# Four Fourier/GEGLU layers: transposed rows through a wide tile and memory, statistics by ScalarE, GELU as one ScalarE function

## The chip, the cores and the metric

The kernel runs on one core of one Trainium2 chip. Such a core has a matmul engine (TensorE, PE in the profile, with its weight load as PEld), VectorE (DVE), ScalarE (ACT), GpSimd (POOL) and SyncE (SP), which here only issues transfers. They work from one on-chip memory of 128 partitions; matmuls write to eight banks of an accumulator (PSUM), and transfers to and from the large memory run on 16 DMA engines. Each engine takes its own instructions in order, and waits on semaphores for the others. The metric is device time in microseconds (us) for one execution; lower is better.

## The reference

A row tensor x of 2048 x 512 passes through four layers. Each normalises its rows (mean and variance over 512, no learned factors) and adds its result to x.

```python
def _A_ref(x, dft_seq_re, dft_seq_im, dft_hid_re, dft_hid_im):      # layers 0 and 2
    a = einsum("bsd,ed->bse", x, dft_hid_re)
    b = einsum("bsd,ed->bse", x, dft_hid_im)
    return einsum("ts,bse->bte", dft_seq_re, a) - einsum("ts,bse->bte", dft_seq_im, b)
def _B_ref(x, w_gate, w_up, w_down):                                # layers 1 and 3
    return (_gelu(x @ w_gate) * (x @ w_up)) @ w_down
x = x + _A_ref(_layernorm(x), ...)
x = x + _B_ref(_layernorm(x), ...)
x = x + _A_ref(_layernorm(x), ...)
x = x + _B_ref(_layernorm(x), ...)
```

The sequence matrices are 2048 x 2048, the hidden ones 512 x 512, the gate and up weights 512 x 1792, the down weights 1792 x 512, all float32. GELU is the tanh form.

## The kernel before, in words

**Precision.** A float32 product is made of three matmuls on a faster type. Each operand is split into a high part (ScalarE copies it to that type, line 110) and a low part (VectorE takes the difference, line 111); `mm3` (lines 144 to 146) multiplies high by high, high by low and low by high into one bank. So nearly every tile that TensorE uses has first passed ScalarE and VectorE, or was stored split.

**Fewer products.** The sequence matrices and the gate/up weights are cut into 2 x 2 blocks and multiplied by Winograd's scheme of seven products in place of eight. The sums and differences of blocks this needs are VectorE's (lines 132 and 135): S1 to S4 on one side, T1 to T4 on the other.

**Layers 0 and 2** (`mix`) work on four blocks `b` of 512 output rows. Stages A11, A12, S2, S3 and A22 multiply sequence tiles by normalised rows; hidden stages then multiply by the hidden matrix, and `x_add` adds x and stores the rows. `plan` gives the order. In each stage of `six`, one step is six matmuls.

**Layers 1 and 3** (`geglu`) work on two halves `w` of 1024 rows, each as two parts of 512. For every `n` of 14 column groups, `up` makes seven products; `finished` applies GELU to the gate (`activated`, lines 719 to 726: square and tanh on ScalarE, two combined operations on VectorE) and multiplies by up. `down_steps` multiplies by the down weights: twelve matmuls each, six of them behind for part 0, and all 14 of part 1 after the ups.

These products need the normalised rows with the 512 features on the partitions, that is, transposed. `block_steps` makes them: `normed` normalises a row tile of 128 x 512 (VectorE statistics, POOL's power -0.5, VectorE's shift, ScalarE's scaling); `turned` (line 450) has TensorE transpose four 128 x 128 pieces into one bank; `first` and `second` copy and split from there, `fourth` and `divide` make and split the T sums.

**Order.** Two mechanisms set it, and a planner that knows assumed durations orders each engine's instructions by them. `items` lists every tile that a product will take, in order; `take` keeps up to five items split (`AHEAD`) and four more loaded (`RAW`) ahead of the product in hand, on SP's queue. `queue` is a list of side work: `step` runs its next entry after each step of the mix or each down step. Into it go the normalisations for the next layer, the transposes, the splitting of down weights (`down_weight_steps`, during layer 0) and of the gate/up weights (`weight_steps`, in layers 0 and 1; six entries a group, of which the first loads and the second sums). Split weights are stored by POOL's queue and read back by SP's.

**Buffers.** All 128 x 512 tiles come from 102 numbered slots (`NSLOT`), given out in the order in which they came free. A load into a slot waits for the slot's last reader. PSUM banks are given out likewise.

## Time and profile before

| | us |
|---|---|
| median of 3 runs | 1665.11 |
| lowest, highest | 1663.8, 1665.39 |
| profiled execution, its own time | 1666.76 |
| span of the profiled execution (first to last instruction) | 1664.9 |

| engine | busy us | share of the span |
|---|---|---|
| TensorE matmul | 1650.4 | 99% |
| TensorE weight load | 1359.2 | 82% |
| VectorE | 1190.7 | 72% |
| ScalarE | 776.2 | 47% |
| GpSimd | 169.3 | 10% |

The mean granted clock of TensorE is 0.998 of full speed. The transfers move 388.46 MB, on average 233 GB/s. How to read it: a busy matmul engine is not one at its best pace, as matmuls are pipelined and their ends are modelled, so a count of matmuls per stretch of time says more than a busy share. In a row of a group, the numbers after the bar are the summed busy time in us, the mean of one in ns, and the idle time of the engine before them with what ended it. In the windows view each row is a stretch of the span. In the view of waits each row is an engine's line, what it waited for, the sum in us, how often, and the longest.

The layers can be placed by the transfers: layer 0 lasts to about 390 us, layer 1 to about 840, layer 2 to about 1240, layer 3 to the end.

### The profile page before, as it was taken

What the parts mean: (1) busy time and instruction counts of PE and PEld (TensorE: products, weight loads), DVE (VectorE), ACT (ScalarE), POOL (GpSimd) and SP (SyncE); (2) the same over time, 40 slices, a digit from 0 to 9 for tenths busy, and PEclk for the clock granted to TensorE, in tenths of its full rate; (3) what the DMA queues carried; (4) which work ended last, traced back from release to release, by engine and by line L of the source; (5) the groups of instructions that cost most, each with busy time, mean ns of one, the idle gap of its engine ahead of it and who ended that gap; (6) DMA issues with size and microseconds to landing.
All of it is one profiled execution on the core that took longest, in us unless ns stands there. A gap on an engine that the chain in (4) does not pass through costs nothing.

```text
span 1664.9 us, 22527 instructions
## 1 busy us (share of the span) xinstructions
PE 1650.4 (99%) x7296; PEld 1359.2 (82%) x7296; DVE 1190.7 (72%) x2132; ACT 776.2 (47%) x1352; POOL 169.3 (10%) x288
## 2 busy tenths in 40 slices
PE   9999999999999999999999999999999999999999
PEld 6877788888788888888888888888888888888887
DVE  8997978687887765655898785857946556656561
ACT  7744434255565543534663333444635443444440
POOL 3212100021422110000210000000100000100000
PEclk9999999999999999999999999999999999999999
DMA  9788886778766876555665766565695559755551
GB/s 361 247 279 329 306 317 227 253 252 291 273 229 215 292 269 233 172 189 198 216 227 182 240 228 228 168 227 188 225 386 184 171 177 321 259 178 175 186 183 51
DMA packets 200726, 388.46 MB, mean 233 GB/s; under 512 B 23840, under 2 KB 27424, under 8 KB 200608
## 3 DMA queue, kind: packets, MB, share of 16 engines
q1 hardware_dynamic: 183168, 329.86, 59.1%
q0 software_dynamic: 17440, 57.16, 9.1%
q8 instruction: 58, 0.95, 0.2%
q14 instruction: 60, 0.49, 0.1%
HBM read 328.73 MB, written 58.20 MB: 232 GB/s over the span
## 4 chain that ended last, share of the span: by engine, by line
PE 93%; DVE 3%; DMA 2%; issue 1%; ACT 1%; SPq 0%; DVEq 0%; ACTq 0%
PE p L144 31%; PE p L145 30%; PE p L146 30%; DMA s<-wgu 2%; DVE s L111 1%; PE p L551 1%; PE p L454 1%; DVE s L135 1%; DMA s<-ws 1%; DVE s L132 1%; DMA s<-x 0%; DVE s L725 0%; DVE s L739 0%; DVE s L723 0%; ACT s L110 0%
## 5 line engine op out<-in xcount | busy, mean ns | idle before, releaser
L145 PE MATMUL p<-s,s 128*128 128x512 f32 x2368 | 921.7, 390 | 1.9 <-DVE s L111 1.9
L146 PE MATMUL p<-s,s 128*128 128x512 f32 x2368 | 908.6, 390 | 0.0
L144 PE MATMUL p<-s,s 128*128 128x512 f32 x2368 | 901.2, 391 | 7.0 <-DVE s L135 3.9
L110 ACT ACTIVATE s<-s 128x512 fp32r<-128x512 f32 (+1 forms) x758 | 438.0, 617 | 467.6 <-DVE s L132 98.6
L111 DVE TENSOR_TENSOR s<-s,s 128x512 fp32r<-128x512 f32 (+1 forms) x758 | 490.2, 679 | 87.1 <-ACT s L110 64.3
L144 PEld LDWEIGHTS p<-s,s 128*128 128x128 f32 x2368 | 445.0, 188 | 102.9 <-DVE s L135 5.0
L145 PEld LDWEIGHTS p<-s,s 128*128 128x128 f32 x2368 | 445.4, 188 | 95.0 <-DVE s L111 3.1
L146 PEld LDWEIGHTS p<-s,s 128*128 128x128 f32 x2368 | 445.2, 188 | 93.7 <-DVE s L111 0.7
L135 DVE TENSOR_TENSOR s<-s,p 128x512 f32<-128x512 f32 x316 | 213.0, 685 | 188.9 <-PE p L146 140.6
L139 ACT ACTIVATE s<-p 128x512 f32<-128x512 f32 x248 | 145.2, 593 | 187.4 <-PE p L146 171.4
L132 DVE TENSOR_TENSOR s<-s,s 128x512 f32<-128x512 f32 (+1 forms) x290 | 172.4, 608 | 23.4 <-DMA s<-ws 15.4
L722 ACT ACTIVATE s<-s 128x512 f32<-128x512 f32 x112 | 70.4, 630 | 91.7 <-DVE s L135 90.9
L725 DVE SCALAR_TENSOR_TENSOR s<-s,s 128x512 f32<-128x512 f32 x112 | 76.8, 690 | 38.2 <-ACT s L724 37.6
L378 POOL TENSOR_TENSOR rstd<-rstd,power 128x1 f32<-128x1 f32 x64 | 50.8, 803 | 506.7 <-DVE rstd L377 500.8
L723 DVE SCALAR_TENSOR_TENSOR s<-s,s 128x512 f32<-128x512 f32 x112 | 77.0, 690 | 33.5 <-ACT s L722 31.3
L724 ACT ACTIVATE s<-s 128x512 f32<-128x512 f32 x112 | 69.5, 627 | 25.0 <-DVE s L723 24.4
L135 DVE TENSOR_TENSOR s<-s,s 128x512 f32<-128x512 f32 (+1 forms) x78 | 50.1, 645 | 38.5 <-DMA s<-ws 22.1
L169 POOL DMA_DIRECT2D x<-s x48 | 26.1, 543 | 443.8 <-DVE s L135 440.8
L382 ACT ACTIVATE s<-s,shift,rstd 128x512 f32<-128x512 f32 x64 | 50.4, 811 | 36.5 <-DVE shift L380 32.1
L739 DVE SCALAR_TENSOR_TENSOR s<-s,s 128x512 f32<-128x512 f32 x84 | 58.0, 690 | 1.6
L197 POOL DMA_DIRECT2D wb<-s x84 | 45.2, 540 | 121.6 <-ACT s L110 85.1
L373 DVE BATCH_NORM_STATS2 st<-s 128x6 f32<-128x512 f32 x64 | 42.7, 689 | 19.8 <-DMA s<-x 19.8
(32 smaller groups left out, 254.6 us busy)
## 6 DMA issues: line engine op xcount, KB each, us to landing
s<-ws SPq DMA_DIRECT2D x432, 256.0 KB, 4.0
s<-wb SPq DMA_DIRECT2D x294, 256.0 KB, 4.1
s<-wd SPq DMA_DIRECT2D x224, 256.0 KB, 4.3
s<-x SPq DMA_DIRECT2D x126, 256.0 KB, 4.1
s<-wh SPq DMA_DIRECT2D x120, 256.0 KB, 4.8
wb<-s POOLq DMA_DIRECT2D x98, 256.0 KB, 3.5
x<-s POOLq DMA_DIRECT2D x48, 256.0 KB, 4.1
wd<-s POOLq DMA_DIRECT2D x28, 256.0 KB, 4.9
```

Source lines behind the costliest of these rows:

```text
L110: nc.scalar.activation(hi, src, AF.Copy)
L111: nc.vector.tensor_tensor(lo, src, f32(hi), op=ALU.subtract)
L132: nc.vector.tensor_tensor(out, a, b, op=ALU.subtract)
L135: nc.vector.tensor_tensor(out, a, b, op=ALU.add)
L139: nc.scalar.activation(v, src, AF.Copy)
L144: nc.tensor.matmul(ps, ah, bh, start=start, stop=False, skip_group_check=True)
L145: nc.tensor.matmul(ps, ah, bl, start=False, stop=False, skip_group_check=True)
L146: nc.tensor.matmul(ps, al, bh, start=False, stop=stop, skip_group_check=True)
L722: nc.scalar.activation(t, g, AF.Square)
L723: nc.vector.scalar_tensor_tensor(t, t, 1.0 / GELU_C, g, op0=ALU.add, op1=ALU.mult)
L724: nc.scalar.activation(t, t, AF.Tanh, scale=GELU_A * GELU_C)
L725: nc.vector.scalar_tensor_tensor(t, t, 1.0, g, op0=ALU.add, op1=ALU.mult)
```

## The change

Six things change together.

1. **Transposes.** TensorE's transposes go. VectorE transposes each normalised row tile in blocks of 32 x 32 into a quarter of a `wide` tile of 128 x 2048 (a pool of one buffer). When four rows are in, POOL's queue stores it to memory (1 MB). Later `fetch` reads it back with SP's queue, so that the features come to stand on the partitions: 32 transfers of 64 KB a block of rows. `first` and `second` split from those tiles; the copies from PSUM go.
2. **Order of rows.** This gives the 512 rows of a part an order of their own: tile n of a part holds four runs of 32 rows, one from each of the part's row tiles. The feed-forward layers load and store x so (`load_rows`, `add_rows` and `last_downs` pass `True` for `mixed`), and x is held in memory as four tensors of 512 rows a layer rather than sixteen of 128. The last four row tiles before layer 2 stay on the chip in that order, so layer 2 reads its last four sequence tiles of each half in it (`seq_tile`).
3. **Statistics.** From layer 1 on, ScalarE makes the sum and the sum of squares about the mean in the passes of a copy and a square, POOL two small operations, ScalarE the shift; layer 0 keeps VectorE's. Eight rows for layer 2 get theirs ahead (`terms_ahead`), during the second half of layer 1.
4. **GELU.** One ScalarE function in place of four operations; the factor 0.5 falls away.
5. **Weights.** Down weights are split at their first use in layer 1 rather than from the queue in layer 0. The loads of gate/up weights are issued a group ahead of the entries that sum and split them. Stored down weights are taken at most two items ahead (`NEAR`), loaded four.
6. **Places in the queue.** In the mix, the norms for the next layer enter in block 2, four in S2 and four in S3, with an empty step between; fetches, splits and T sums stay in the last block. In the feed-forward layers, a step of the queue also runs after every product, and the next half's rows enter before the last six downs of part 0. Slots: 98, so that the wide tile finds room.

```diff
-NSLOT = 102
+NSLOT = 98
...
-    nc.scalar.activation(warm, warm, AF.Tanh)
+    nc.scalar.activation(warm, warm, AF.Gelu_apprx_tanh)
...
+    def rows(layer, i, mixed=False):
+        g, n = divmod(i, NT)
+        if mixed:
+            return xs[layer, g].rearrange("(n j t) d -> j n t d", n=NT, t=32)[n]
+        return xs[layer, g][n * P:(n + 1) * P]
+
+    def x_load(layer, i, mixed=False):
         t = sb.get()
-        nc.sync.dma_start(t, xs[layer, i])
+        nc.sync.dma_start(t, rows(layer, i, mixed))
...
-        engine.dma_start(xs[layer + 1, i], t)
+        engine.dma_start(rows(layer + 1, i, mixed), t)
...
+            if stream["loaded"] > n + NEAR and items[stream["loaded"]][2] is whole:
+                break
...
+            if items[stream["split"]][2] is whole and stream["split"] > n + NEAR:
+                break
...
+    def make_down_first(f):
+        def run(v):
+            p = plain(v)
+            kept(wds[f], p)
+            return p
+        return run
...
+    def seq_tile(layer, n, k):
+
+        if layer and k >= NS - NT:
+            return ws[(n + 1) * NS - NT:(n + 1) * NS, (k % NT) * 32:(k % NT + 1) * 32]
+        return ws[n * NS + k]
...
+    def norm_terms(layer, i, x, junk):
+
+        pool = spool if layer == 0 else kpool
+        rstd = pool.tile([P, 1], F32, name="rstd")
+        shift = pool.tile([P, 1], F32, name="shift")
+        if layer == 0:
+            st = spool.tile([P, 6], F32, name="st")
+            nc.vector.bn_stats(st, x)
+            mv = spool.tile([P, 2], F32, name="mv")
+            nc.vector.bn_aggr(mv, st)
+            nc.vector.tensor_scalar_add(rstd, mv[:, 1:2], EPS)
+            nc.gpsimd.tensor_tensor(rstd, rstd, power, op=ALU.pow)
+            nc.vector.scalar_tensor_tensor(shift, mv[:, 0:1], -1.0, rstd, op0=ALU.mult, op1=ALU.mult)
+        else:
+
+            total = spool.tile([P, 1], F32, name="total")
+            mean = spool.tile([P, 1], F32, name="mean")
+            nc.scalar.activation(junk, x, AF.Copy, accum_out=total)
+            nc.scalar.activation(mean, total, AF.Copy, scale=-1.0 / D)
+            nc.scalar.activation(junk, x, AF.Square, bias=mean, accum_out=rstd)
+            nc.gpsimd.tensor_scalar(rstd, rstd, 1.0 / D, EPS, op0=ALU.mult, op1=ALU.add)
+            nc.gpsimd.tensor_tensor(rstd, rstd, power, op=ALU.pow)
+            nc.scalar.activation(shift, mean, AF.Copy, scale=rstd)
+        return rstd, shift
+
+    def terms_ahead(layer, i):
+        x, junk = x_load(layer, i), sb.get()
+        known[layer, i] = norm_terms(layer, i, x, junk)
+        sb.put(x, junk)
...
+                z = normed(layer, w * 2 * NT + i)
+                part, n = divmod(i, NT)
+                if n == 0:
+                    wide[part] = tpool.tile([P, NT * D], F32, name="wide")
+                to = wide[part].rearrange("p (b n t) -> p b n t", n=NT, t=32)
+                nc.vector.transpose(to[:, :, n], z.rearrange("p (b t) -> p b t", t=32))
+                sb.put(z)
+                if n == NT - 1:
+                    nc.gpsimd.dma_start(turned[part], wide.pop(part))
             return run
 
-        def turned(c, part):
-
-            ps = ps8.get()
-            for i in range(NT):
-                nc.tensor.transpose(ps[:, i * P:(i + 1) * P], z[part * NT + i][:, c * P:(c + 1) * P], ident)
-            if c == ND - 1:
-                sb.put(*(z.pop(part * NT + i) for i in range(NT)))
-            return ps
+        def fetch(c):
+
+            def run():
+                for part in range(2):
+                    v = zt[c, part] = sb.get()
+                    for i in range(P // 32):
+                        cols = turned[part][:, (c * 4 + i) * P:(c * 4 + i + 1) * P]
+                        to = v[i * 32:(i + 1) * 32]
+                        nc.sync.dma_start(
+                            to.rearrange("p (j t) -> p j t", t=P), cols.rearrange("(j p) t -> p j t", p=32)
+                        )
+            return run
...
+                v = t[f"B{1 + c // 2}1", c % 2] = zt.pop((c, 0))
+                blocks[f"B{1 + c // 2}1", c % 2] = split_slot(v)
...
-        one = [norm(i) for i in range(NT)] + [first(c) for c in range(ND)]
-        two = [norm(i) for i in range(NT, 2 * NT)] + [second(c) for c in range(ND)]
+        one = [norm(i) for i in range(2 * NT)]
+        two = [fetch(c) for c in range(ND)] + [first(c) for c in range(ND)] + [second(c) for c in range(ND)]
...
+            if b == NB - 2:
+                norms, others = block_steps(layer + 1, 0)
+                queue.extend([run for norm in norms[:NT] for run in (norm, None)])
+                rest.extend((norms[NT:], others))
...
-                queue.extend(weight_steps(0))
+                opening_weights.update((n, weight_steps(n)) for n in range(2))
+                queue.extend([opening_weights[0][0], None, opening_weights[1][0], None, *opening_weights[0][1]])
...
-                queue.extend(block_steps(layer + 1, 0))
+                queue.extend(rest[1])
                 if layer == 0:
-                    queue.extend(weight_steps(1))
+                    queue.extend(opening_weights[1][1])
+            if b == NB - 2:
+                queue.extend([run for norm in rest[0] for run in (norm, None)])
...
-        nc.scalar.activation(t, g, AF.Square)
-        nc.vector.scalar_tensor_tensor(t, t, 1.0 / GELU_C, g, op0=ALU.add, op1=ALU.mult)
-        nc.scalar.activation(t, t, AF.Tanh, scale=GELU_A * GELU_C)
-        nc.vector.scalar_tensor_tensor(t, t, 1.0, g, op0=ALU.add, op1=ALU.mult)
+        nc.scalar.activation(t, g, AF.Gelu_apprx_tanh)
...
-                nc.vector.scalar_tensor_tensor(t, t, 0.5, v, op0=ALU.mult, op1=ALU.mult)
+                nc.vector.tensor_tensor(t, t, v, op=ALU.mult)
...
+            if n + 3 in making:
+                making[n + 3][0]()
+            if n + 2 in making:
+                queue.extend(making[n + 2][1])
...
+            for k in range(NK):
+                queue.extend([lambda k=k: terms_ahead(layer + 1, k), *[None] * 7])
...
+        if w == 0:
+            queue.extend(run for part in block_steps(layer, 1) for run in part)
+        elif before_mix:
             queue.extend((lambda k=k: first_rows(layer + 1, k)) for k in range(NK))
+            for k in range(NT):
+                queue.append(lambda k=k: second_rows(layer + 1, k))
+                queue.append(lambda k=k: combine(k))
+            queue.extend((lambda k=k: combine_late(k)) for k in range(NT))
...
-    for run in [run for f in range(NF) for run in down_weight_steps(f)]:
-        queue += [run, None, None]
```

More of the change, by code (lines that the diff above doesn't have):

```diff
@@ L354, in fnet_geglu @@
         mix_items(layer)
-        for _ in range(NB // 2):
-            items.extend((F32R, halves(wds[f]), lambda *w: w, None) for _ in range(2) for f in range(NF))
+        for w in range(NB // 2):
+            for part in range(2):
+                for f in range(NF):
+                    if layer == w == part == 0:
+                        items.append((F32, (wdn[f],), make_down_first(f), None))
+                    else:
+                        items.append((F32R, halves(wds[f]), whole, None))
     queue = []
@@ L381, in normed @@
+    def terms_ahead(layer, i):
+        x, junk = x_load(layer, i), sb.get()
+        known[layer, i] = norm_terms(layer, i, x, junk)
+        sb.put(x, junk)
+    def normed(layer, i):
+        x = row_of(layer, i)
         z = sb.get()
+        rstd, shift = known.pop((layer, i), None) or norm_terms(layer, i, x, z)
         nc.scalar.activation(z, x, AF.Identity, bias=shift, scale=rstd)
@@ L689, in divide @@
             return run
-        return [load, sums] + [divide(i) for i in range(len(pieces))]
-    def down_weight_steps(f):
-        raw = []
-        def load():
-            raw.append(sb.get())
-            with tc.issue_after(stream["last"].ins):
-                nc.sync.dma_start(raw[0], wdn[f])
-        def store():
-            p = plain(raw[0])
-            kept(wds[f], p)
-            sb.put(*p)
-        return [load, store]
+        return load, [sums] + [divide(i) for i in range(len(pieces))]
     def weight_load(n):
@@ L760, in down_steps @@
             sb.put(*hs, *v)
-        making = layer == 1 and w == 0
+        making = {}
+        if layer == 1 and w == 0:
+            making.update((n, weight_steps(n)) for n in range(2, NF))
+            making[2][0]()
         chain, side, c11, u, w4 = {}, {}, {}, {}, {}
         def product(n, ps, an, bn, start, stop):
-            if making:
-                step()
+            step()
             hi, lo = wparts[n][an]
@@ L825, in up @@
             sb.put(*wparts.pop(n)["tiles"])
-            if making and n + 3 < NF:
-                queue.extend(weight_steps(n + 3))
-            elif not making and n + 2 < NF:
+            if not making and n + 2 < NF:
                 weight_load(n + 2)
```

84 lines of the change are left out of this document (35 added, 49 removed).

## The prediction

> **What bounds the kernel now.** I read the page from the top: busy shares, then the chain that ended last.
>
> ```profile
> span 1664.9 us, 22527 instructions
> ## 1 busy us (share of the span) xinstructions
> PE 1650.4 (99%) x7296; PEld 1359.2 (82%) x7296; DVE 1190.7 (72%) x2132; ACT 776.2 (47%) x1352; POOL 169.3 (10%) x288
> ...
> ## 4 chain that ended last, share of the span: by engine, by line
> PE 93%; DVE 3%; DMA 2%; issue 1%; ACT 1%; SPq 0%; DVEq 0%; ACTq 0%
> ```
>
> TensorE is busy 99% and holds 93% of the chain. So what counts is work that leaves TensorE, and the few places where TensorE waits. A busy row can hide a slow pace, so I took two pieces of the chain in order of time for the price of one instruction:
>
> ```profile
> 98.99 0.91 PE p L144 x4
> ...
> 603.06 0.88 PE p L454 x8
> ```
>
> A product matmul costs 0.91/4 = 0.227 us, a transpose (line 454) 0.88/8 = 0.11 us. With 0.227 us known, a count of matmuls in 25 us shows lost time even where busy hides it. These are the stretches below the full count (the 575 row is a full one), and two that matter for DVE and DMA; columns are PE, PEld, DVE, ACT, POOL busy with counts, granted clock, DMA share, GB/s.
>
> ```profile
> core 0: us, PE busy (x) PEld busy (x) DVE busy (x) ACT busy (x) POOL busy (x), PEclk, DMA share, GB/s
> 75.00:100.00 25.00, 24.17 (x107) 19.67 (x106) 25.00 (x42) 10.74 (x21) 3.24 (x6) 1.00 0.90 311
> 100.00:125.00 25.00, 24.42 (x108) 19.92 (x107) 23.92 (x41) 13.56 (x24) 5.41 (x10) 1.00 0.75 259
> 125.00:150.00 25.00, 23.88 (x106) 19.43 (x105) 20.78 (x34) 12.00 (x22) 4.85 (x9) 1.00 0.80 274
> 200.00:225.00 25.00, 22.70 (x94) 18.36 (x93) 19.63 (x33) 11.23 (x21) 4.32 (x8) 0.93 0.78 277
> 350.00:375.00 25.00, 23.98 (x114) 19.72 (x113) 21.57 (x47) 11.56 (x20) 2.46 (x4) 1.00 0.69 233
> 425.00:450.00 25.00, 22.12 (x89) 17.30 (x88) 19.32 (x39) 12.77 (x24) 9.63 (x18) 0.93 0.79 279
> 550.00:575.00 25.00, 24.82 (x109) 20.01 (x108) 19.79 (x35) 16.20 (x31) 2.70 (x5) 1.00 0.83 283
> 575.00:600.00 25.00, 25.00 (x112) 20.69 (x111) 16.34 (x36) 9.11 (x15) 3.82 (x7) 1.00 1.05 390
> 850.00:875.00 25.00, 25.00 (x112) 20.71 (x111) 23.26 (x46) 20.43 (x38) 2.15 (x5) 1.00 0.77 245
> 1050.00:1075.00 25.00, 25.00 (x112) 20.69 (x111) 25.00 (x42) 11.90 (x21) 0.00 (x0) 1.00 0.39 131
> ```
>
> A full stretch starts 112 matmuls. Lost time by (112 - x) x 0.227: 1.1, 0.9, 1.4, 4.1, 5.2 and 0.7 us at 75, 100, 125, 200, 425 and 550; at 350 the count is mixed with transposes, so there I take the 1.0 us that busy lacks. Together 14.4 us. The two big ones have a granted clock of 0.93: a wait of about 2.3 us is followed by a stretch of reduced clock, so a wait costs nearly twice itself. What TensorE waited for:
>
> ```profile
> PE p L144 <- DVE s L135: 3.9, 3, 2.3
> PE p L144 <- ACT s L139: 2.5, 3, 1.9
> PE p L145 <- DVE s L111: 1.9, 2, 1.1
> ...
> 436.98 0.43 DVE L135 TENSOR_TENSOR s<-s,s 128x256 f32<-128x256 f32 x1 [4.68 <-DMA s<-wgu]
> ```
>
> Always results of VectorE or ScalarE. The last row shows why near 440 us: VectorE stood 4.68 us for a gate/up weight that was loaded too late, with what TensorE needed queued behind it.
>
> **The change part by part.** Prices of the pieces:
>
> ```profile
> L111 DVE TENSOR_TENSOR s<-s,s 128x512 fp32r<-128x512 f32 (+1 forms) x758 | 490.2, 679 | 87.1 <-ACT s L110 64.3
> L110 ACT ACTIVATE s<-s 128x512 fp32r<-128x512 f32 (+1 forms) x758 | 438.0, 617 | 467.6 <-DVE s L132 98.6
> L722 ACT ACTIVATE s<-s 128x512 f32<-128x512 f32 x112 | 70.4, 630 | 91.7 <-DVE s L135 90.9
> L725 DVE SCALAR_TENSOR_TENSOR s<-s,s 128x512 f32<-128x512 f32 x112 | 76.8, 690 | 38.2 <-ACT s L724 37.6
> L723 DVE SCALAR_TENSOR_TENSOR s<-s,s 128x512 f32<-128x512 f32 x112 | 77.0, 690 | 33.5 <-ACT s L722 31.3
> L724 ACT ACTIVATE s<-s 128x512 f32<-128x512 f32 x112 | 69.5, 627 | 25.0 <-DVE s L723 24.4
> L373 DVE BATCH_NORM_STATS2 st<-s 128x6 f32<-128x512 f32 x64 | 42.7, 689 | 19.8 <-DMA s<-x 19.8
> L382 ACT ACTIVATE s<-s,shift,rstd 128x512 f32<-128x512 f32 x64 | 50.4, 811 | 36.5 <-DVE shift L380 32.1
> L378 POOL TENSOR_TENSOR rstd<-rstd,power 128x1 f32<-128x1 f32 x64 | 50.8, 803 | 506.7 <-DVE rstd L377 500.8
> L454 PE MATMUL p<-ident,s 128*128 128x128 f32 x128 | 17.0, 272 | 0.0
> ...
> L80 ACT ACT_TABLE_LOAD x1 | 1.3, 1283 | 0.7 <-PEq L974 0.7
> ...
> 195.39 0.33 SPq L210 DMA_DIRECT2D s<-ws  x1
> ...
> s<-ws SPq DMA_DIRECT2D x432, 256.0 KB, 4.0
> s<-wd SPq DMA_DIRECT2D x224, 256.0 KB, 4.3
> x<-s POOLq DMA_DIRECT2D x48, 256.0 KB, 4.1
> out<-s SPq DMA_DIRECT2D x4, 256.0 KB, 2.0
> ```
>
> *Transposes leave TensorE.* All 128 go: 128 x 0.11 = 14 us of the engine that sets the end, between matmuls, hidden by nothing. Taken: -13.9; bounds -12 and -14.1.
>
> *What replaces them.* 32 rows of z (16 per feed-forward layer) get a VectorE transpose in 32x32 blocks. The trace has none; every 128x512 VectorE row lies at 0.68 to 0.69 us, so 32 x 0.69 = 22 us, at most double that. Then 8 stores of 1 MB by POOL and 128 fetches of 64 KB by SP. At 0.33 us an issue the fetches hold SP for 42 us in all, 2.6 us for each of 16 queued steps of eight. The two megabytes of one block move in 2 x 1.05/0.39 = 5.4 us of all DMA engines, perhaps twice that in pieces of 512 bytes. They are queued behind their store and, on SP, ahead of weight and sequence tiles. Those are split five items ahead of use, 5 x 6 x 0.227 = 6.8 us, and loaded at least four more ahead, 12.2 us; a landing takes 4.0 us, so some 8 us of delay stay hidden. In the last block of the mix the fetches come when one tile is loaded every 2.7 us, so SP has room. In the feed-forward stage norms start six down steps earlier than before. Cost taken 0. If the cover goes, the next product waits for VectorE, whose queue stands at a split.
>
> The single wide buffer makes the fifth norm's transpose wait for the first store. Behind it on VectorE are splits. In the mix the halves are 16 steps apart (22 us); in the feed-forward stage one down step (12 x 0.227 = 2.7 us), and VectorE would stand there 2.7 + 4.1 - 2.7 = 4 us (a megabyte's transfer and a landing, less the step). TensorE then lives on parts split earlier. Counted in the new waits below.
>
> *GELU.* Two VectorE operations vanish (77.0 + 76.8 = 154 us) and one of two on ScalarE (70 us, at the same 0.63 us for the new one, which the trace does not show; bounds 0.6 and 1.3). All beside TensorE, so 0 directly; but it empties VectorE in the stage of 425 to 552 us.
>
> *Statistics by ScalarE* in 48 of 64 norms: minus 48 x 0.689 = 33 us VectorE, plus 48 x 2 x 0.62 = 60 us ScalarE and some short operations, and a second POOL operation of 0.8 us. The added wait: the shift on ScalarE stands behind two POOL steps, 1.6 us, with splits behind it. VectorE ends near 1190 - 154 - 33 + 22 = 1025 us, ScalarE near 776 - 70 + 60 = 770 plus the short ones. Neither nears the span.
>
> *Down weights* leave layer 0 (14 splits, 28 stores, with their loads) and are split at first use in layer 1. In 100 to 225 us VectorE loses 14 x 0.68 = 9.5 us of work. That is where 0.9 + 1.4 + 4.1 = 6.4 us were lost. Taken -5.4. The first 75 to 100 us keep VectorE at 25.00 of 25; nothing there goes, so 1.1 us stays.
>
> *Gate/up loads* move a whole group of seven products ahead of their sums (over 9 us, against the 4.68 us wait). Taken: all 5.2 us at 425 go, and with 0.8 of the 1.7 at 350 and 550, -6.0.
>
> *Rows in mixed order.* Feed-forward rows are loaded and stored as four pieces of 32 rows, and layer 2 reads 64 sequence tiles so. Same bytes. Final store: 0 to +2 us; taken +1, as it is the only transfer at the end that nothing covers (2.0 us now).
>
> [...]
>
> *New waits.* At the start of layer 2 four rows (lines 406, 410) are normalised in successive steps: per step 0.62 x 2 + 0.81 + two splits of 0.62 = 3.3 us of ScalarE against 1.36, so it falls 4 x 1.9 = 7.7 us behind; five split items cover 6.8. The row at 850 shows ScalarE at 20.43 already. Price 0 to 0.9 + as much at reduced clock. Four fewer slots shorten the loads' lead most in the sum-heavy steps, where VectorE is at 25.00 of 25 (1050 row). Bounds for all of these 0 and +13 (three waits like the ones at 200 and 425, at 4 to 5 us). Taken +2.3: TensorE lost nothing from 575 on, even with VectorE full, so I stay near the lower end.
>
> **Sum.** -13.9 - 5.4 - 6.0 + 1 + 2.3 = -22.0. The profiled execution took 1666.76 us, so 1644.8; it stands 1.65 us above the median of 1665.11, so 1643 us.
>
> **The rivals.**
>
> *A. Transposes go, but waits come in their place.* VectorE is relieved, yet the down weights, the 42 us of fetch issue and the wide buffer meet in the feed-forward stage at 590 to 650 us and its twin in layer 3. For it: DMA is full there (1.05 share). Against: 25.00 busy today. Four waits at 4 us in place of my 2.3: 1643 + 16 - 2.3 = 1657 us.
>
> *B. Slower: mixed tiles on few DMA engines.* If a transfer in four pieces runs on a quarter of the engines, 256 KB take 4 x 0.256 x 1.05/0.39 = 2.8 us instead of 0.7. Layer 2 reads such tiles in 16 groups of four, in the A12 and A22 steps one per 1.36 us: four of them fall 4 x 1.4 = 5.8 us behind. With 8 us of cover that is hidden; once the lead falls below 4.0 + 5.8 = 9.8 us, each group waits. It decides against the change from 22/16 = 1.4 us a group; at 2 us plus the slower clock, 16 x 3.5 = 56 us, so 1643 + 56 - 1 = 1698 us. [...]
>
> *C. The waits stay.* Only the transposes count: 1665.1 - 13.9 + 1 = 1652 us, if the 200 us wait belongs to the sums rather than to the down weights.
>
> *D. Table loads.* One load (1.28 us) in the run covers square, tanh, copy and identity. If the new function and Square lay in different tables, 48 x 2 x 1.28 = 123 us of ScalarE would come in pairs of 2.6 us, mostly under cover; 1643 + 48 x 0.4 = 1662 us if 0.4 us of each shows. [...]
>
> **How the numbers follow.** Forecast (1637 to 1649): 0.55. A: 0.18. C: 0.13. D: 0.03. B: 0.09. Remainder 0.02 within 0.2%, which is about what a measurement here can tell from no change. Faster holds forecast, A, C and most of D: 0.88; same 0.03; slower, B: 0.09. Range 1636 to 1659: the forecast, C and A; below it little is possible, since -13.9 - 14.4 gives 1637.
>
> **What would show it.** Line 454 gone, 32 VectorE transposes near 0.69 us; the counts at 200 and 425 us back at 112 with clock 1.00; VectorE near 1025 us; one table load; a landing of mixed rows near 4 us. Wrong if any stretch after 575 us falls under 112 matmuls with a clock below 1.00, if mixed rows land in over 8 us, or if ScalarE waits for POOL while TensorE waits for a split.

## The result, and the profile after

The changed kernel takes 1848.51 us (median; 1846.1 to 1857.6) against 1665.25 us: a ratio of 1.111, interval 1.107 to 1.1149. The forecast was a gain of 22 us; the loss is 183 us. The ends of the profile's page, first the busy shares, then the chain that ended last and the rows of the new operations:

```profile
span 1844.3 us, 22260 instructions
...
PE 1689.5 (92%) x7168; PEld 1372.9 (74%) x7168; DVE 1030.4 (56%) x1748; ACT 782.1 (42%) x1504; POOL 191.9 (10%) x344
...
PE 52%; issue 19%; DMA 17%; DVE 5%; ACT 4%; SPq 1%; POOL 1%; DVEq 0%; ACTq 0%; POOLq 0%
...
L786 ACT ACTIVATE s<-s 128x512 f32<-128x512 f32 x112 | 70.1, 629 | 122.7 <-DVE s L138 121.8
...
L515 DVE STREAM_TRANSPOSE wide<-s 128x512 f32<-128x512 f32 x32 | 22.2, 704 | 27.7 <-ACT s L443 15.9
```

The parts cost what was priced: 704 ns a transpose on VectorE, 629 ns for the new GELU, VectorE at 1030 us (1025 was worked out). Yet TensorE's share of the chain fell from 93% to 52%; DMA stands there with 17%, and 19% is "issue", time for which the profile shows no releaser. The windows show where:

```profile
200.00:225.00 25.00, 25.00 (x112) 20.71 (x111) 18.51 (x30) 10.07 (x18) 0.00 (x0) 1.00 0.73 239
350.00:375.00 25.00, 20.89 (x81) 16.71 (x80) 22.19 (x39) 9.96 (x17) 0.59 (x2) 0.86 0.68 200
425.00:450.00 25.00, 25.00 (x112) 20.72 (x111) 18.89 (x38) 11.87 (x23) 12.26 (x24) 1.00 0.91 328
625.00:650.00 25.00, 13.14 (x41) 9.37 (x42) 4.06 (x7) 5.73 (x16) 1.48 (x4) 0.76 0.55 158
1100.00:1125.00 25.00, 15.96 (x63) 13.12 (x64) 11.36 (x18) 7.27 (x12) 0.00 (x0) 0.75 0.55 163
1125.00:1150.00 25.00, 25.00 (x112) 20.69 (x111) 8.44 (x13) 5.01 (x9) 2.16 (x4) 1.00 0.67 210
1350.00:1375.00 25.00, 12.01 (x38) 9.24 (x37) 14.31 (x24) 8.13 (x15) 0.00 (x0) 0.63 0.78 241
```

At 200 and 425 us the two stalls of before are gone, as forecast. At 625, 1100 and 1350 no compute engine is full, and the DMA engines are busy to 0.55 to 0.78 on average: everybody waits for something that moves slowly. The chain, piece by piece, in layer 2 (start, length, what):

```profile
1091.73 0.23 PE p L149
1092.26 14.69 DMA s<-ws
1107.03 0.64 ACT s L113
1107.73 0.57 issue
1108.30 0.69 DVE s L138
1109.04 0.80 PE p L147
1109.83 0.43 PE p L148
1110.26 0.43 PE p L149
...
1113.14 0.23 PE p L147
...
1139.68 13.86 DMA s<-ws
```

A matmul ends and frees a slot, a sequence tile is loaded into it, and lands 14.69 us later, where before the median landing took 4.0. In the chain of the kernel before, the longest rows of sequence tiles are:

```profile
77.26 5.42 DMA s<-ws
...
117.57 4.80 DMA s<-ws
```

In the chain after, ScalarE and VectorE then work on the tile, and TensorE starts again at 0.43 us a matmul instead of 0.23 for some 3.5 us.

Matmuls come in the same order in both kernels, so their starts in the trace of the profiled execution give the time of each stage (worked out from those starts; us; layer 0 from its first matmul; the last column is from VectorE's last operation to the end of the span). The runs named below stand beside it. By these starts layer 0 of the kernel before ends at 415 us, not at about 390 as its transfers suggested.

| | layer 0 | 1, half 0 | 1, half 1 | layer 2 | 3, half 0 | 3, half 1 | end |
|---|---|---|---|---|---|---|---|
| before | 407.3 | 218.9 | 209.4 | 395.5 | 213.1 | 209.4 | 2.9 |
| after | 410.1 | 217.1 | 230.2 | 536.6 | 209.4 | 223.8 | 8.8 |
| x1, sequence tiles whole | 408.7 | 220.4 | 230.8 | 431.1 | 209.4 | 225.6 | |
| x2, four pieces of 32 rows | 408.8 | 218.7 | 209.9 | 407.9 | 209.4 | 217.3 | |
| x3, before with 64 mixed tiles | 403.6 | 218.1 | 209.4 | 488.7 | 213.1 | 209.4 | |
| x4, no mixed rows | 406.5 | 209.4 | 220.3 | 407.3 | 209.4 | 210.5 | 3.2 |
| x6, x4 without terms ahead | 407.4 | 209.4 | 210.8 | 399.3 | 209.4 | 210.1 | |
| x11, before with 98 slots | 409.9 | 219.4 | 209.4 | 400.0 | 213.2 | 209.4 | |

After against before: +141.1 in layer 2, +20.8 and +14.4 in the second halves, +5.9 at the end, +2.8, -1.8 and -3.7 elsewhere: +179.5, and the spans differ by 1844.3 - 1664.9 = 179.4 us.

### The profile page after: what moved, and what is told of

It reads as the page before. It is cut to its first block, busy times and chain, and to the rows that moved or that the text cites. A ratio compares the mean times of both kernels' runs of the same rounds, so it can differ in the third digit from the quotient of the medians.

```text
span 1844.3 us, 22260 instructions
## 1 busy us (share of the span) xinstructions
PE 1689.5 (92%) x7168; PEld 1372.9 (74%) x7168; DVE 1030.4 (56%) x1748; ACT 782.1 (42%) x1504; POOL 191.9 (10%) x344
## 4 chain that ended last, share of the span: by engine, by line
PE 52%; issue 19%; DMA 17%; DVE 5%; ACT 4%; SPq 1%; POOL 1%; DVEq 0%; ACTq 0%; POOLq 0%
PE p L148 17%; PE p L147 17%; PE p L149 17%; DMA s<-ws 7%; DMA s<-x 5%; DVE s L114 3%; ACT s L113 2%; DMA s<-wd 1%; DMA x<-s 1%; DMA s<-wh 1%; DVE s L135 1%; DVE s L138 1%; ACT s L428 1%; DMA s<-t 1%; SPq L529 1%
## 5 line engine op out<-in xcount | busy, mean ns | idle before, releaser
L147 PE MATMUL p<-s,s 128*128 128x512 f32 x2368 | 919.9, 399 | 109.5 <-ACT s L113 49.6
L148 PE MATMUL p<-s,s 128*128 128x512 f32 x2368 | 940.3, 398 | 33.8 <-DVE s L114 31.2
L149 PE MATMUL p<-s,s 128*128 128x512 f32 x2368 | 924.3, 396 | 0.7 <-DVE s L114 0.7
L113 ACT ACTIVATE s<-s 128x512 fp32r<-128x512 f32 (+1 forms) x782 | 454.6, 617 | 609.8 <-DMA s<-ws 129.4
L147 PEld LDWEIGHTS p<-s,s 128*128 128x128 f32 x2368 | 454.9, 193 | 217.5 <-ACT s L113 71.9
L148 PEld LDWEIGHTS p<-s,s 128*128 128x128 f32 x2368 | 455.3, 192 | 139.8 <-DVE s L114 41.9
L149 PEld LDWEIGHTS p<-s,s 128*128 128x128 f32 x2368 | 454.0, 192 | 97.2 <-DVE s L114 1.6
L138 DVE TENSOR_TENSOR s<-s,p 128x512 f32<-128x512 f32 x316 | 211.2, 683 | 278.6 <-PE p L149 210.5
L142 ACT ACTIVATE s<-p 128x512 f32<-128x512 f32 x224 | 129.9, 592 | 161.3 <-PE p L149 153.2
L786 ACT ACTIVATE s<-s 128x512 f32<-128x512 f32 x112 | 70.1, 629 | 122.7 <-DVE s L138 121.8
L800 DVE TENSOR_TENSOR s<-s,s 128x512 f32<-128x512 f32 x84 | 57.8, 689 | 2.1 <-ACT s L786 0.3
L429 POOL TENSOR_SCALAR rstd<-rstd 128x1 f32<-128x1 f32 x48 | 14.3, 298 | 425.4 <-ACT s L428 393.6
L426 ACT ACTIVATE s<-s 128x512 f32<-128x512 f32 x48 | 29.8, 622 | 63.2 <-DMA s<-x 63.1
L515 DVE STREAM_TRANSPOSE wide<-s 128x512 f32<-128x512 f32 x32 | 22.2, 704 | 27.7 <-ACT s L443 15.9
L800 DVE TENSOR_TENSOR s<-s,p 128x512 f32<-128x512 f32 x28 | 19.2, 685 | 28.3 <-PE p L149 28.3
L428 ACT ACTIVATE s<-s,mean 128x512 f32<-128x512 f32 x48 | 34.2, 712 | 0.3
## 6 DMA issues: line engine op xcount, KB each, us to landing
s<-ws SPq DMA_DIRECT2D x432, 256.0 KB
s<-wb SPq DMA_DIRECT2D x294, 256.0 KB
s<-wd SPq DMA_DIRECT2D x196, 256.0 KB
s<-x SPq DMA_DIRECT2D x134, 256.0 KB
s<-wh SPq DMA_DIRECT2D x120, 256.0 KB
wb<-s POOLq DMA_DIRECT2D x98, 256.0 KB, 3.8
x<-s POOLq DMA_DIRECT2D x48, 256.0 KB, 6.6
```

Of the source, the lines that this page charges most:

```text
L113: nc.scalar.activation(hi, src, AF.Copy)
L138: nc.vector.tensor_tensor(out, a, b, op=ALU.add)
L142: nc.scalar.activation(v, src, AF.Copy)
L147: nc.tensor.matmul(ps, ah, bh, start=start, stop=False, skip_group_check=True)
L148: nc.tensor.matmul(ps, ah, bl, start=False, stop=False, skip_group_check=True)
L149: nc.tensor.matmul(ps, al, bh, start=False, stop=stop, skip_group_check=True)
```

## The experiments

Theory B: the transfers in mixed order (rows in four runs of 32) are slow because they run on four DMA engines. Rival theories: the new waits (statistics, terms ahead, the wide tile, fetches), or the lost slots.

**x1: layer 2's sequence tiles whole again.** The last four rows are loaded in their own order; the feed-forward layers stay mixed.

```diff
-        if layer and k >= NS - NT:
-            return ws[(n + 1) * NS - NT:(n + 1) * NS, (k % NT) * 32:(k % NT + 1) * 32]
         return ws[n * NS + k]
...
-            add_rows(1, before_mix)
+            add_rows(1)
```

> The changed kernel, but layer 2 reads its last four rows back from memory in their own order, so that its 64 sequence tiles are transfers of 128 whole rows again; the 36 mixed transfers of x by SP and 28 by POOL stay. Theory B (a transfer in four pieces runs on four of sixteen DMA engines, and layer 2 starves): layer 2, 537 us in the changed kernel, comes back to 395 to 405, in all 1848 - 135 = 1705 to 1720 us. Rival A (new waits from statistics on ScalarE, the fetches and the wide buffer): layer 2 stays over 500 us, the whole over 1810.

Measured: 1746.29 us, ratio 1.0487 (1.0466 to 1.0508). Layer 2 went from 536.6 to 431.1 us; the second halves stayed where they were. That is less than theory B had forecast, but far from rival A. So 105 us hang on these 64 transfers, or on what they make late. Of the 36 us that layer 2 still has over the kernel before, 29 lie in its second and third stage (worked out from the matmul starts): there the four rows are read back from memory, which this edit brings with it, after POOL's mixed stores of them.

**x3: the same 64 transfers alone, in the kernel before.** The order of the rows stays as it was, so layer 2 pairs tiles and rows that don't belong together; the work is the same.

```diff
+    def seq_tile(layer, n, k):
+
+        if layer and k >= NS - NT:
+            return ws[(n + 1) * NS - NT:(n + 1) * NS, (k % NT) * 32:(k % NT + 1) * 32]
+        return ws[n * NS + k]
...
-            rows = [[ws[(b * 2 + m) * NS + k] for k in range(NS)] for m in range(2)]
+            rows = [[seq_tile(layer, b * 2 + m, k) for k in range(NS)] for m in range(2)]
```

> The kernel before, with one thing of the change: layer 2 reads its last four sequence tiles of each half in the mixed order, 64 transfers in four pieces (its rows stay in the old order, so the sum of layer 2 pairs the wrong rows). Theory B: layer 2 rises from 395 to some 500 to 540 us, in all 1770 to 1810. Rival A: unchanged, 1665.

Measured: 1757.57 us, ratio 1.0554 (1.0533 to 1.0576), all of it in layer 2: 395.5 to 488.7 us, a little under the forecast of theory B. So 64 transfers of 1490, with the same bytes, cost 93 us, or 93/16 = 5.8 us for each group of four. The line of packets, and its chain:

```profile
DMA packets 199958, 388.46 MB, mean 221 GB/s; under 512 B 23072, under 2 KB 26656, under 8 KB 199840
...
942.94 0.23 PE p L146
943.25 11.56 DMA s<-ws
...
983.39 10.78 DMA s<-ws
```

The same line of the kernel before:

```profile
DMA packets 200726, 388.46 MB, mean 233 GB/s; under 512 B 23840, under 2 KB 27424, under 8 KB 200608
```

The kernel before issues 1490 transfers (1272 by SP, 218 by POOL) and has 16 x 1490 = 23840 packets under 512 bytes: sixteen a transfer. The run has 768 fewer, which is 64 x 12, so four for each of the 64. Read as one such packet for each engine of a transfer, each of the 64 ran on four engines instead of sixteen. The load of the DMA engines agrees: in the changed kernel from 1838 to 1840 us, where only two of its last mixed stores are under way, the two together keep them busy to 0.25, a quarter of the sixteen, and move 98 GB/s. The trace shows the same in the semaphore on which a transfer reports: in the kernel before every transfer of SP makes 16 arrivals there, and in x3 these 64 make five, one about a microsecond after the issue and four at the landing (counted from the semaphore times of the trace). In the changed kernel 100 transfers of SP make five: the 64, 32 loads of x and the last four stores.

**x2: each mixed transfer as four of 32 whole rows.** Same bytes in the same places.

```diff
...
+        places = rows(layer, i, mixed)
+        for to, place in zip(pieces_of(t, len(places)), places):
+            nc.sync.dma_start(to, place)
...
-            return ws[(n + 1) * NS - NT:(n + 1) * NS, (k % NT) * 32:(k % NT + 1) * 32]
+            return [ws[(n + 1) * NS - NT + m, (k % NT) * 32:(k % NT + 1) * 32] for m in range(NT)]
...
```

> The changed kernel with every mixed transfer issued as four transfers of 32 rows; the same bytes in the same order, three more issues of about 0.33 us each. Theory B: sixteen engines again, so layer 2 falls to about 400 us and the starts of the second halves of layers 1 and 3 (230 and 224 us) lose most of their 35 us of stall: 1640 to 1665 us. Rival A: the stalls stay, 1800 or more. If only the queue of SP were too busy, it would get worse, by up to 300 x 0.33 us.

Measured: 1691.64 us, ratio 1.0155 (1.0132 to 1.0178), over the expected range of 1640 to 1665. Its rows of issues:

```profile
s<-ws SPq DMA_DIRECT2D x368, 256.0 KB, 4.0
...
s<-ws SPq DMA_DIRECT2D x256, 64.0 KB, 2.5
```

A piece lands in 2.5 us, a whole tile in 4.0 as before, and 157 of the 183 us are back. Since only the pattern of the transfers changed, the order of rows as such costs little: it was the pattern. What is left (+26 us) belongs to the other parts, and to four issues where there was one.

**x4: no mixed rows at all.** x and the sequence tiles are read whole, and the order is put right on chip, by the access pattern of a split that is made anyway.

```diff
...
-                h[f, part] = split_slot(t)
+                hi, lo = h[f, part] = sb.get(F32R), sb.get(F32R)
+                out = "p (n j t) -> p n j t"
+                split(
+                    t.rearrange("p (j n t) -> p n j t", n=NT, t=32),
+                    hi.rearrange(out, n=NT, t=32),
+                    lo.rearrange(out, n=NT, t=32),
+                )
...
```

> The changed kernel with no mixed rows at all: the order of the rows is put right where the product of gate and up is split for the down product, by the access pattern of that copy and that difference. 64 sequence tiles, all x rows in 128 whole rows. Theory B: like the run with four pieces or a few us better, 1635 to 1655 us, and faster than the kernel before. Rival A: 1800 or more. If the pattern of 32-element runs slows ScalarE and VectorE to double, 0.6 us more on each for 112 tiles, under cover.

Measured: 1678.01 us, ratio 1.0087 (1.0067 to 1.0107). That is over the expected 1635 to 1655. So mixed rows cost 170 us of the 183, but of the forecast's gain nothing is left, although the transposes are gone. The largest wait that is left lies in the second half of layer 1; its window, ScalarE's waits for x in the whole run, and the chain there:

```profile
625.00:650.00 25.00, 18.15 (x65) 13.06 (x64) 16.00 (x26) 12.24 (x25) 2.97 (x6) 0.86 0.93 322
...
ACT s L424 <- DMA s<-x: 43.7, 12, 13.3
...
633.59 7.63 DMA s<-x
641.31 0.73 ACT s L424 x2
642.27 0.49 ACT s L142
642.80 0.80 PE p L147
```

Line 424 is the first pass of ScalarE's statistics. It stood up to 13.3 us for a row of x, with other work queued behind it. That longest wait ended at 619.5 us, while TensorE still had work. The one in the chain, 7.0 us of idle ScalarE until 641.31, held TensorE: a copy out of a bank (line 142), for which the next product waits, stood behind it. Both are for rows whose statistics are made ahead.

**x6: x4 without the terms ahead.** The eight rows get their statistics with their norm.

```diff
-        if before_mix:
-            for k in range(NK):
-                queue.extend([lambda k=k: terms_ahead(layer + 1, k), *[None] * 7])
```

> The run without mixed rows (1678 us), only without the eight rows whose terms ScalarE makes ahead in the second half of layer 1; ScalarE then makes them at the end of that half. Theory S: that half goes from 220 back to some 210 us, layer 2's start gains nothing or loses some, in all 1666 to 1672 us. Rival F: 220 us stay, 1676 to 1680.

Measured: 1663.76 us, ratio 0.9991 (0.998 to 1.0001), under the expected range. The second half of layer 1 went from 220.3 to 210.8 us, layer 2 from 407.3 to 399.3. That is the best of all versions, and still not to be told from the kernel before. Where the terms ahead cost their time depends on the rest: x2 has them too, and loses in layer 1's first half (218.7) what x4 loses in the second.

**x5: x4 with VectorE's statistics everywhere** (and so no terms ahead).

```diff
...
-        if layer == 0:
+        if True:
...
-        if before_mix:
-            for k in range(NK):
-                queue.extend([lambda k=k: terms_ahead(layer + 1, k), *[None] * 7])
```

> The run without mixed rows (1678 us), with VectorE's statistics in all layers and without the rows whose terms were made ahead. Theory S (what is left over the forecast is statistics on ScalarE: loads it waits for in order, POOL's two steps, and splits queued behind): the second half of layer 1 loses its 11 us of stall and layer 2 most of its 12, so 1655 to 1662 us. Rival F (the fetches on SP's queue, or 98 slots in place of 102): 1672 to 1680.

Measured: 1666.85 us, ratio 1.0007 (0.9994 to 1.0019), between its two forecasts. Layer 0, where the norms for layer 1 fall into steps with a full VectorE, took 414.5 us against 407.4 in x6. But the intervals of x5 and x6 overlap, so it is not shown that statistics on ScalarE help; what hurt in x4 was making them ahead.

**x9 and x7: GELU alone.** x9 is the kernel before with the new function; x7 is x4 with the four operations.

```diff
...
-        nc.scalar.activation(t, g, AF.Square)
-        nc.vector.scalar_tensor_tensor(t, t, 1.0 / GELU_C, g, op0=ALU.add, op1=ALU.mult)
-        nc.scalar.activation(t, t, AF.Tanh, scale=GELU_A * GELU_C)
-        nc.vector.scalar_tensor_tensor(t, t, 1.0, g, op0=ALU.add, op1=ALU.mult)
+        nc.scalar.activation(t, g, AF.Gelu_apprx_tanh)
...
```

> The kernel before with one part of the change, GELU as one ScalarE function. The wait at 440 us is for a gate/up weight that lands late, so it should stay: 1660 to 1666 us. If VectorE's load was the cause of it, 1657 to 1660.

> The run without mixed rows (1678 us), with GELU as four operations again (154 us back on VectorE, 70 us on ScalarE). If GELU as one function is worth nothing on the path, 1676 to 1681 us; if VectorE's load in the feed-forward stages delays products, 1682 to 1695, with the loss in the first half of layer 1 where gate/up weights are split.

Measured: x9 1664.24 us, ratio 0.9992 (0.9978 to 1.0006); x7 1673.78 us, 1.0052 (1.0035 to 1.0069), 4 us below x4 rather than at or above it, so under both of its forecasts, and why is open. In x9 VectorE falls from 1190.7 to 1050.9 us and the time does not move:

```profile
PE 1649.9 (99%) x7296; PEld 1358.8 (82%) x7296; DVE 1050.9 (63%) x1908; ACT 715.9 (43%) x1240; POOL 167.5 (10%) x288
```

**x11: the kernel before with 98 slots.**

```diff
-NSLOT = 102
+NSLOT = 98
```

> The kernel before, with 98 data slots in place of 102 and nothing else changed. Theory S (the four slots that the wide tile takes shorten the lead of the loads, and that is what the kernel without terms ahead still loses in the S2 steps: 3 us in layer 0's block 0, 2 to 3 us in blocks 2 and 3, 1.5 and 3.2 us in layer 2's blocks 1 and 2): the kernel before shows the same stalls in S2, 4 to 8 us in all, 1669 to 1673 us. Rival (the losses come from ScalarE's statistics and from norms in block 2's S2, not from the slots): S2 keeps its pace, 1664 to 1667 us.

Measured: 1674.28 us, ratio 1.0053 (1.0039 to 1.0067). So theory S holds, a little above its range: four slots of 102 cost some 9 us, with +2.6 in layer 0 and +4.5 in layer 2 by the table. In layer 0 the S2 steps of blocks 0 and 3 lose 2.7 and 4.7 us more than before. At the same time layer 0's stalls in its last A12, first S3 and second hidden stage (1.1, 1.4 and 4.1 us in the kernel before) are gone.

**x12, x13, x14: the slots back, and norms later.** x12 is x6 with four ordinary slots, held only while four rows are gathered, in place of the wide tile, and 102 slots. x13 puts all eight norms of block 2 into its S3 steps as well. x14 does that alone, with the wide tile. Of the two excerpts below, the first belongs to x12 and x13, the second to x13 and x14.

```diff
...
-                    wide[part] = tpool.tile([P, NT * D], F32, name="wide")
-                to = wide[part].rearrange("p (b n t) -> p b n t", n=NT, t=32)
-                nc.vector.transpose(to[:, :, n], z.rearrange("p (b t) -> p b t", t=32))
+                    wide[part] = [sb.get() for _ in range(ND)]
+                for c, v in enumerate(wide[part]):
+                    to = v.rearrange("p (b n t) -> p b n t", n=NT, t=32)
+                    nc.vector.transpose(to[:, :, n], z[:, c * P:(c + 1) * P].rearrange("p (b t) -> p b t", t=32))
...
-                norms, others = block_steps(layer + 1, 0)
-                queue.extend([run for norm in norms[:NT] for run in (norm, None)])
-                rest.extend((norms[NT:], others))
+                rest.extend(block_steps(layer + 1, 0))
...
```

> The kernel with the order put right in the split and no terms ahead, and in place of the one wide tile four ordinary slots that are held only while four rows are gathered (four 128x128 transposes a row in place of one 128x512, four stores of 256 KB in place of one of 1 MB), with 102 slots again. Theory S: the S2 stalls go, 1652 to 1659 us, under the kernel before for the first time by more than it varies. Rival: no change from 1663.8, 1661 to 1666 us.

> As the run with the slots back, and the eight norms of the next layer's first block all in block 2's S3 steps, none in its S2, where VectorE is full. If norms in S2 cost the 2 to 3 us that block 2's S2 loses, 2 to 5 us under that run in S2 of block 2 of both mixes; if slots alone are the cause, the same time within 1.5 us; slower by 2 us or more if S3 has no room for eight norms.

> The kernel with the order put right in the split, no terms ahead, the one wide tile and 98 slots, and the eight norms of the next layer's first block all in block 2's S3 steps, none in its S2. There 2.0 us (layer 0) and 3.2 us (layer 2) were lost in S2. If norms in a VectorE-bound stage cost that, 1658 to 1661 us, against 1663.8 with four norms in S2. If the lost slots alone do it, or S3 and the next S2 lose as much, 1662 to 1666 us.

Measured: x12 1677.96 us, ratio 1.007 (1.0057 to 1.0083); x13 1673.27 us, 1.0043 (1.0031 to 1.0056); x14 1665.83 us, 1.0001 (0.9988 to 1.0013). x12 missed both of its forecasts; x14 lies in the range of its second branch, that S3 and what follows lose as much as S2 wins. In x12 the S2 steps before the norms do recover their pace, as the slots theory says (layer 0's block 0 from 24.8 to 21.8 us, layer 2's block 1 from 23.3 to 21.8, which is the pace without a wait). But S2 of layer 2's block 2, where the rows are gathered, takes 32.0 us instead of 25.0, and more is lost than won. x13 brings that step to 21.8 us, but loses a part of it again in other steps and ends 4.7 us under x12. In x14 S2 of that block takes 21.8 us, and S3 and A22 behind it lose 3.0 and 2.8 more: the wait moved. Which part of the gathering (four transposes, four stores, or four slots asked for at once) costs x12 its time was not tried apart.

## Why the prediction was wrong, step by step

**Transposes, -13.9: right.** Layer 3's first half takes 209.4 us in place of 213.1, after and in x4 and x6: 3.6 us of transposes. The first half of layer 1 has as many, and S3 and A22 of the last block of layers 0 and 2, where the others stood, are about 3.5 us shorter (layer 0 in x14, layer 2 in x6; worked out from the matmul starts). The 512-byte pieces of the fetches took 27 ns in the median against 84 for pieces of 2048 (packets in the trace of the changed kernel): 1.3 times as long a byte, where the forecast allowed for twice.

**Down weights, -5.4: the stalls went, the cause isn't shown.** The stalls of layer 0's last A12, first S3 and second hidden stage (1.1 + 1.4 + 4.1 = 6.6 us) are gone after. But they are gone in x11 too, where the down weights stay in layer 0, and x3, whose edit touches layer 2 alone, has only 3.6 us of them. And layer 0 gained nothing in all: 407.3 us before, 410.1 after, 406.5 in x4, as its S2 steps lose what the others won.

**Gate/up loads, -6.0: right in place and size.** The ups of layer 1's first half took 160.9 before, 156.2 after and 155.0 in x4, which is 5.9 us less; in x11, with the loads as before, 161.4.

**GELU, 0: right.** x9 shows it without anything else: VectorE's relief of 140 us is worth nothing there.

**Final store, +1 (0 to +2): too small.** It is 5.9 us. From VectorE's last operation to the end of the span were 2.9 us, and are 8.8. The rows, first before, then after:

```profile
1661.31 0.69 DVE s L135
```

```profile
1834.79 0.69 DVE s L138
```

It is the one place in which the slow transfer stands bare. The last store itself lands 7.7 us after its issue instead of 2.0 (semaphore times of the trace); the stores before it, 5.9, 7.2 and 7.9.

**Rows in mixed order, 0 beyond that store: the step that failed.** The prediction put these transfers at nothing because they carry the same bytes and 8 us of their landing would stay hidden. Between after and x4 they cost 169.0 us of span. Rival B named the mechanism, as a supposition that no trace showed then and x3 shows now, and priced it at 55 us with a chance of 0.09. Its price of one transfer holds. While TensorE stands in x3, the DMA engines are busy to 0.26 and move 98 GB/s, and at that rate the 0.262 MB of a tile take 2.7 us (2.8 was worked out):

```profile
953.00:955.00 2.00, 0.00 (x0) 0.00 (x0) 0.00 (x0) 0.10 (x1) 0.00 (x0) 0.50 0.26 98
```

But the landing and the cover were wrong.

First, the landing. A transfer of 2.8 us on four engines was spread over the steps of its group, so that four tiles fell 5.8 us behind. In the runs the four are issued close together and land one behind another. In the chain above they were issued at 1088.9, 1089.5, 1091.0 and 1092.3 us, and landed at 1095.7, 1098.2, 1101.9 and 1107.0 (semaphore times of the trace): 18.1 us from the first issue to the last landing. If all queue on the same four engines, 4 x 2.8 + 4.0 = 15 us (an estimate). That the four tiles took the same four engines was not read from a run; the share of 0.25 for two mixed stores at once, at the end of the changed kernel, speaks for it. The median landing of the 64 is 8.2 us in x3 and 8.8 after. Whole tiles behind them come late too: the 13.86 us of the chain above are one with 16 arrivals.

Second, the cover. "loaded at least four more ahead, 12.2 us" is the plan's number, and 8 us of it were counted as free. A load needs a slot, and the slots come back from readers. The waits of the kernel before show it, in SP's and ScalarE's rows rather than in TensorE's:

```profile
SPq L210 <- PE p L146: 311.8, 201, 7.9
SPq L210 <- DVE s L111: 157.5, 107, 6.8
...
ACT s L110 <- DMA s<-ws: 58.3, 34, 4.5
```

SP held item loads 308 times until a reader had freed the slot, and ScalarE already stood 34 times, up to 4.5 us, for a sequence tile of 4.0 us. The lead was partly spent before the change. SP also waits for transfers still under way: for sequence tiles 18.5 us in all before, 55.5 in x3.

Nor does the lead run to the product that uses the tile. The four late tiles of the chain above are, by the order of the loads, the last four of A22, and TensorE stands at A22's first step. What it waits for is a sum that VectorE makes (line 138), and in VectorE's order the split of the last late tile (line 114) stands before it:

```profile
1107.69 0.69 DVE L114 TENSOR_TENSOR s<-s,s 128x512 fp32r<-128x512 f32 x1 [4.37 <-ACT s L113]
1108.30 1.28 DVE L138 TENSOR_TENSOR s<-s,p 128x512 f32<-128x512 f32 x2
```

The prediction names this path for the fetches (the next product waits for VectorE, whose queue stands at a split) and doesn't apply it to the mixed tiles. In x3 three such waits, at the ends of S3, make 36 of the 93 us; TensorE's row for them in the time of layer 2:

```profile
PE p L144 <- DVE s L135: 35.7, 3, 13.8
```

In x3, with 102 slots and no other edit, a group costs 5.8 us; after, with 98 slots and the other parts, (536.6 - 407.3)/16 = 8.1 us. These are means of very unequal groups: by stage, x3's 93 us lie in S3 (45.5), S2 (25.5), A12 (15.4) and A22 (6.7), worked out from the matmul starts, while B had looked at A12 and A22. B's threshold of 1.4 us a group was right, and the groups lay far beyond it on average.

The same transfers bring x into the feed-forward layers and take it out. They make up most of the 14 us in layer 3's second half (13.3 between after and x4), 9.9 of the 20.8 in layer 1's, and 7.7 us in layer 1's first half, which hide there behind what other parts won. TensorE's own waits after show the ways by which it comes through:

```profile
PE p L147 <- ACT s L113: 49.6, 15, 8.8
PE p L147 <- DVE s L138: 31.8, 3, 14.8
PE p L148 <- DVE s L114: 31.2, 14, 6.7
PE p L147 <- ACT s L142: 13.0, 3, 6.5
PE p L147 <- DMA s<-wh: 13.0, 1, 13.0
```

The engine named is mostly the last link; behind it stands ScalarE, for a tile:

```profile
L113 ACT ACTIVATE s<-s 128x512 fp32r<-128x512 f32 (+1 forms) x782 | 454.6, 617 | 609.8 <-DMA s<-ws 129.4
```

**New waits, +2.3 (0 to +13): too small as well, and enough by itself to lose the gain.** Without mixed rows, x4's span is 1675.3 us. The steps above give 1664.9 - 14.2 (transposes) - 6.6 (stalls of layer 0) - 5.9 (ups) = 1638.2; so 37 us of new waits. Taking out the terms ahead gives 14 us of them back (1678.0 to 1663.8); the forecast had looked for ScalarE's lag at the start of layer 2 and not for the waits for x that they bring into layer 1, and layer 2 itself is 8.0 us faster without them. Four slots cost 9 us where nothing else is changed (x11); the forecast named them and took a share of 2.3. If these add up, some 14 us are left. x6 loses them in S2 and S3 steps of both mixes; x12 to x14 moved them about and did not take them away, and their cause stays open; x14 speaks against a simple one, that norms in S2 are at fault. That x12, with all 102 slots, is slower than x6 says that the slots' 9 us can't simply be added. The wait for the one wide tile came about as priced (in x4 VectorE stood 5.74 us for its first store near 590 us; 4 were worked out) and cost nothing there: that half runs at 209.4 us.

**Rival A** (waits in the feed-forward stage at 590 to 650 us) was right in place, at 625 us, and its 16 us near what x4 shows there (10.9 us in layer 1's second half), but by luck: it blamed the down weights, the fetches and the wide tile, and x6, which has all three, runs that half in 210.8 us. **D** (table loads) fell: after has one load of 1.28 us, as before, though its ScalarE runs the new function, square, copy and identity. **C**'s time didn't come; the stall at 200 us is gone in every version that has the change's weight steps, but in x11 too, so what it hung on stays open.

At least two of the three signs that the prediction named against itself came: stretches after 575 us under 112 matmuls with clocks of 0.63 to 0.76, and mixed rows landing in over 8 us. The third, ScalarE waiting for POOL, came nine times after, up to 3.9 us each; whether TensorE stood for it was not read.

## What to carry to other kernels

Look at the access pattern of a transfer as at its bytes: here the same 256 KB, cut into four runs of 32 rows, ran on four DMA engines instead of sixteen on SP's queue and cost 5.8 us a group of four on average; four transfers (x2), or a reordering inside a split that is made anyway (x4), brought 157 and 170 of the 183 us back. Don't take the lead of a load from the plan: read in the waits of the loading queue and of the first reader how much of it is still there, and look at what stands behind that reader's instruction in its engine's order. And where TensorE holds 93% of the chain, taking 140 us off VectorE was worth nothing (x9), while four buffers of 102 were worth 9 us (x11).

## What the runs showed of the hardware that was not expected

The engines of a transfer on SP's queue could be counted here from the packets under 512 bytes (16 x 1490 before, POOL's included, and 12 fewer for each mixed transfer in x3). The page of the changed kernel has no landing for SP's queue at all ("s<-ws SPq DMA_DIRECT2D x432, 256.0 KB", with no time), so the chain or the semaphore times had to give it.

POOL's stores in mixed order suffer too, but the count doesn't tell their engines: each still makes 16 arrivals, and POOL's queue has 5376 packets more after than in x4, 192 for each of its 28 mixed stores. Rows of after, which were 4.1 and 4.3 before and 4.7 and 5.1 in x4:

```profile
x<-s POOLq DMA_DIRECT2D x48, 256.0 KB, 6.6
...
out<-s POOLq DMA_DIRECT2D x12, 256.0 KB, 10.3
```

Only 16 of the 48 in the first row are mixed; those take 9.1 us in the median (semaphore times), against 4.0 in x4.

An access pattern with runs of 32 elements on both sides cost ScalarE and VectorE little in a split: x4's ScalarE total is 783.8 us against 782.1 after, and VectorE's 1028.9 against 1030.4.
